# Forgetting attention and SiLU feed-forward on one core: score matmuls grouped by head pair, and PSUM banks and second-layer pieces reassigned

## The chip, the cores and the metric

The kernel runs on one core of a Trainium2 chip. A core has a matrix engine (TensorE, in profiles PE for matmuls and PEld for weight loads), a vector engine (VectorE, DVE), an activation engine (ScalarE, ACT), GpSimd (POOL), and SyncE (SP), which here only issues DMAs. Each engine works through its own queue in program order and waits on semaphores. Matmul results go to PSUM, eight banks of 128 partitions by 2 KB; all else lies in SBUF.

The metric is device microseconds for one execution, inputs and outputs in DRAM. Less is better. The time before is 346.61 us, the median of 6 runs (345.94 to 347.65).

## The reference, cut to what matters

Batch 8, 8 heads, sequence 576, head size 64; then a feed-forward layer of 512 to 2048 to 512 over all 4608 tokens.

```python
scores = scale * np.matmul(q, k.transpose(0, 1, 3, 2))
log_f = np.log(np.clip(f, 0.0001, 1.0))
cum = np.cumsum(log_f, axis=-1)
decay = cum[:, :, :, None] - cum[:, :, None, :]
scores = np.where(causal, -1000000000.0, scores + decay)
attn = softmax(scores)                      # over the last axis
attn_out = np.matmul(attn, v)
x = attn_out.transpose(0, 2, 1, 3).reshape(B * S, H * D)
h = x @ w_in
out = (h * (1.0 / (1.0 + np.exp(-h)))) @ w_out
```

## The kernel before, in words

**Decay.** The row part of the decay cancels in the softmax, so only a weight by key is left. It is multiplied into v (`convert_v`, on POOL), which has one more column for the denominator.

**Attention units.** A unit `n` is a pair of heads of one batch: 32 units, `NU`. Queries 0 to 127 of every head are done in an opening part (`turn0`, `scores0`, `out0`, `back0`). The pair loop at the end (`for m in range(NQ)`, line 832) does queries 128 to 575, two units an iteration, and it is what the change touches. For a unit, `cast_qk` (POOL) makes bf16 copies, and `transposes` (a DMA transpose on SP's queue) makes `qkT` with head size on the partitions: 64 rows for each of the two heads, so that two score matmuls use the upper and lower half of the array at once ("64*128" in the profile).

**Scores.** The score blocks of a unit are split in three chunks, `CHUNKS[0..2]`, each up to 512 columns a head. A chunk of both heads takes a tile `sc` of two banks of the pool `psc` (2 buffers, so 4 banks). ScalarE takes the exponential into `u`; for chunk 2 also into `ut`, which holds the 64 tail queries. VectorE multiplies the diagonal blocks by the causal masks `tri` (line 469) and `trit` (line 483). In an iteration the chunks come in three groups: `(n,0) (n,1)`, then `(n,2) (n+1,0)`, then `(n+1,1) (n+1,2)`.

**Attention output.** `attend(n)` multiplies `u` and `ut` with v into a tile `dn` of one bank, of the pool `pbig` (4 buffers of one bank); VectorE divides by the denominator into `xr`. `back(m)` turns the two units' `xr` into columns of `x`, by TensorE transposes (`tx`) for the first four pairs and the last, by DMA on SP's queue for the others.

**Feed-forward.** The tokens are split into groups `g` of 256 to 512. M1 chunk `(g, fc)` (`m1_chunk`) is four matmuls into a `pbig` bank `hp`; ScalarE takes the tanh (line 576), VectorE makes `gt` from it and `hp` (line 577), which sets the bank free. M2 piece `(g, tb, part)` (`m2_part`) is four matmuls of 512 columns into a `pbig` bank `po`; four pieces make one tile of 128 tokens, so the bank is held across them. ScalarE copies it to `osb` and POOL's queue stores it. M2 of a group needs all of the group's M1.

**Order.** The order of every engine's work is that of the program text (a manual schedule). Between attention steps, `slot(t)` calls `fill(t)`, which emits M1 and M2 pieces for about `t` us of TensorE work. `step` chooses: it compares how far M1 of the next group and M2 of the present one are, alternates when they are close, and takes M1 first near the end of a group. `two_more` in the opening part also uses `fill`. After each `slot`, `store` issues the outputs of earlier slots. `prepare(n)`, before each of the first two slots, emits the casts, transposes and loads for units `n + 2` and `n + 4`.

The third argument of `fill` before is `least`; its second, `first`, says which kind comes first.

Of the kernel before, what the change touches and what calls it, by code (L numbers as in the profile page):

```python
# [18 lines left out]
def kernel(  # L19
# [22 lines left out]
    RB = NR * P  # L42
# [9 lines left out]
    scale = 1.0 / float(D) ** 0.5  # L52
# [7 lines left out]
    upool = ctx.enter_context(tc.tile_pool(name="upool", bufs=4))  # L60
# [16 lines left out]
    tri = const.tile([P, P], BF16, name="tri")  # L77
# [13 lines left out]
    NG = len(GW)  # L91
# [341 lines left out]
    T0 = P  # L433
# [11 lines left out]
    def scores(n, c):  # L445
        b, p = divmod(n, NP)
        if c == 0:
            us[n] = upool.tile([P, 2, UW], BF16, name="u", tag="u")
        u, ut = us[n], uts[n % 4]
        t = qkT[n]  # L450
        sc = psc.tile([P, 2, SM], FP32, name="sc", tag="sc")
        for kb, q0, q1, o in CHUNKS[c]:
            for i in range(2):
                r = slice(i * D, (i + 1) * D)
                if kb == 0:
                    kt = kT0[b][r, p, :]
                else:
                    k0 = RB if kb == NM else kb * P + RB
                    kt = t[r, k0 : k0 + P]
                nc.tensor.matmul(  # L460
                    sc[:, i, o : o + q1 - q0], lhsT=kt, rhs=t[r, q0:q1], start=True, stop=True
                )
        w = SM if c < 2 else T0
        nc.scalar.activation(  # L464
            out=u[:, :, c * SM : c * SM + w], in_=sc[:, :, 0:w], func=ACT.Exp, scale=scale
        )
        if c == 0:
            x = u[:, :, 0:RB].rearrange("p i (a t) -> p i a t", t=P)
            nc.vector.tensor_tensor(  # L469
                out=x,  # L470
                in0=x,
                in1=tri[:, None, None, :].to_broadcast([P, 2, NR, P]),
                op=ALU.mult,
            )
        if c == 2:
            nc.scalar.activation(  # L476
                out=ut[:, :, 0:3:2, :].rearrange("p k i t -> p i k t"),
                in_=sc[:, :, T0 : T0 + (NM + 1) * ST].rearrange("p i (k t) -> p i k t", t=ST),
                func=ACT.Exp,
                scale=scale,  # L480
            )
            x = ut[:, NM, 0:3:2, :]
            nc.vector.tensor_tensor(  # L483
                out=x, in0=x, in1=trit[:, None, :].to_broadcast([P, 2, ST]), op=ALU.mult
            )

    NGR = 2 * NR + 1

# [2 lines left out]
    def attend(n):  # L491
        b, p = divmod(n, NP)
        if p % 2 == 0:
            xqs[n // 2] = xqp.tile([P, NGR, 2, D], BF16, name="xr", tag="xr", bufs=3)
        xq = xqs[n // 2]
        u, ut = us.pop(n), uts[n % 4]
        dn = pbig.tile([P, NGR, D + 1], FP32, name="dn", tag="big")

        def vals(kb, i):
            h = head(p, i)  # L500
            return v0[b][:, h, :] if kb == 0 else vbf[b][:, kb - 1, h, :]

        for i in range(2):
            for c in range(1, NM):
                for kb in range(c + 1):
                    o = AT[c, kb]
                    nc.tensor.matmul(  # L507
                        dn[:, i * NR + c - 1, :],
                        lhsT=u[:, i, o : o + P],
                        rhs=vals(kb, i),  # L510
                        start=(kb == 0),
                        stop=(kb == c),
                    )
# [117 lines left out]
    M2 = []  # L631
# [4 lines left out]
    at = {"m1": 0, "m2": 0, "left": 0.0, "last": 0, "row": 0}  # L636
    ready: set[int] = set()
    open2 = {"w": False}

    def step():  # L640

        a, c = at["m1"], at["m2"]
        can1 = a < len(M1) and M1[a][0] in ready
        g1 = M1[a][0] if a < len(M1) else NG
        g2 = M2[c][0] if c < len(M2) else NG
        if can1 and M1[a][1] == 0 and g1 > g2 + 1:
            can1 = False
        can2 = open2["w"] and c < len(M2) and g2 < g1
        if not can1 and not can2:
            return None  # L650
        if can1 and can2:
            f1 = M1[a][1] / NFC
            f2 = (c - sum(M2_OF[:g2])) / M2_OF[g2]
            want = 3 - at["last"] if abs(f1 - f2) < 0.15 else (1 if f1 < f2 else 2)
            if want == at["last"] and at["row"] >= 2 and abs(f1 - f2) < 0.25:
                want = 3 - want
            if sum(M2_OF[: g2 + 1]) - c <= 2 and f1 >= 0.75:
                want = 1
            can1 = want == 1
        kind = 1 if can1 else 2  # L660
        at["row"] = at["row"] + 1 if kind == at["last"] else 1
        at["last"] = kind
        if can1:
            m1_chunk(*M1[a])
            at["m1"] += 1
            return 4 * (GW[g1] / 2.4 + 2.5)
        m2_part(*M2[c])
        at["m2"] += 1
        return 4 * (DM / 2.4 + 2.5)
# [6 lines left out]
    def fill(us_, first=0, least=0):  # L676
        if first:
            at["last"], at["row"] = 3 - first, 2
        at["left"] += us_ * 1000
        while at["left"] > 0 or least > 0:  # L680
            t = step()
            if t is None:
                at["left"] = 0.0
                return False
            at["left"] -= t
            least -= 1
        return True

# [79 lines left out]
    def two_more(b, banned):  # L768
        for x in range(2):
            turn0(b + x, 0)  # L770
            turn0(b + x, 1)
            fill(0.6, 0, 1)
        for x in range(2):
            if banned:
                scores0(b + x, ban0(b + x))
            else:
                scores0(b + x)
                mask0(b + x)
            fill(0.6 if x == 0 else 2.0, 2, 1 if x == 0 else 2)
        out0(b)  # L780
        fill(0.6, 0, 1)
        out0(b + 1)
        fill(0.8, 0, 2)
        back0(b, on_act)
        fill(0.6, 0, 1)
        back0(b + 1, on_act)
        fill(0.6, 2, 1)

    fill(5.0)
    two_more(4, True)  # L790
    ready.add(1)
    fill(5.0)
    open2["w"] = True
    fill(6.0, 2)
    two_more(6, False)
    ready.add(2)
    fill(4.0)
# [22 lines left out]
    LAG = 13.0  # L820
    pending: list = []

    def slot(us_, first=0):
        n = len(stores)
        fill(us_, first)
# [66 lines left out]
```

The softmax here doesn't subtract the row's maximum and nothing guards it: scores larger than these inputs give would overflow.

## Time and profile before

| What | Value |
|---|---|
| median of 6 runs | 346.61 us |
| the profiled execution | 345.94 us |
| its span, first to last instruction | 344.2 us |
| mean granted TensorE clock | 0.999 |
| DMA traffic, mean | 147 GB/s |
| M2 matmuls, line 613 | 592, 144.7 us |
| M1 matmuls, line 568 | 832 in all forms |
| pair-loop scores, line 460 | 768 matmuls |
| exponentials of 1024 columns, line 464 | 64, mean 1034 ns |
| tanh of 384 columns, line 576 | 128, mean 503 ns |
| gt of 384 columns, line 577 | 128, mean 553 ns |
| copies po to osb of 512 columns, line 623 | 35, mean 607 ns |
| pair-loop scores, first and last group start | 60.37 and 272.34 us |

The profile is of one execution. The span is 1.7 us shorter than the execution's time, which includes what lies around the instructions. The listed length of a matmul reaches to the end of its pipeline; matmuls overlap, so the time that one takes of TensorE is the difference between its start and that of the next. Instructions of one kind in a row are merged in the timeline, with their count behind an x. In square brackets stands the idle time of the engine before an instruction, and what ended it.

### The profile page before, as it was taken

The numbers are of one execution on the slowest core, as the hardware profiler recorded it, in microseconds if no ns is written. First come the engines' busy times: TensorE is split into PE (matmuls) and PEld (weight loads), VectorE is DVE, ScalarE is ACT, GpSimd is POOL, SyncE is SP. The second block draws the span as 40 slices with busy tenths as digits, with TensorE's granted clock in tenths as the row PEclk, the third lists the DMA queues.
The fourth block names the chain that finished last, engine by engine and source line by source line (L and its number), as shares of the span: only waits on it lengthen the run. The fifth ranks groups of instructions, "written<-read, shape, count | busy, mean of one in ns | idle before, by whom it ended". The sixth has DMA issues, their size and how long they took to land.

```text
span 344.2 us, 8892 instructions
## 1 busy us (share of the span) xinstructions
PE 335.3 (97%) x3567; PEld 199.2 (58%) x3567; DVE 183.7 (53%) x389; ACT 218.1 (63%) x401; POOL 129.5 (38%) x227
## 2 busy tenths in 40 slices
PE   8999999989998999999999999999999999999995
PEld 3754656657655656466465665656656565555664
DVE  4766635465667467367545654546645454535330
ACT  5867555887586766756759667595775934445441
POOL 8996224834526363155127128225320000010011
PEclk9999999999999999999999999999999999999999
DMA  8999999999699897998889799989932000010113
GB/s 152 197 192 218 199 165 159 229 215 196 155 196 195 197 200 155 177 201 182 162 185 175 169 180 196 161 190 173 172 86 57 33 32 30 32 58 28 39 39 85
DMA packets 141497, 50.44 MB, mean 147 GB/s; under 512 B 132368, under 2 KB 138768, under 8 KB 141456
## 3 DMA queue, kind: packets, MB, share of 16 engines
q1 hardware_dynamic: 131440, 32.70, 54.4%
q0 software_dynamic: 9856, 17.04, 21.1%
q8 instruction: 28, 0.46, 0.6%
q10 hardware_dynamic: 160, 0.13, 0.1%
q14 instruction: 13, 0.11, 0.1%
HBM read 36.85 MB, written 9.44 MB: 134 GB/s over the span
## 4 chain that ended last, share of the span: by engine, by line
PE 72%; DMA 15%; SPq 4%; POOL 4%; issue 2%; ACT 1%; DVE 1%; POOLq 0%
PE po L613 30%; PE hp L568 28%; PE sc L460 6%; DMA kf<-in_k_dram 5%; PE dn L507 4%; DMA vf<-in_v_dram 4%; DMA w_out_bf<-in_moe_w_out_dram 3%; PE dn L516 2%; SPq L158 2%; DMA qkb<-in_k_dram 1%; DMA qkT<-qkb 1%; SPq L428 1%; POOL qkb L131 1%; DMA qf<-in_q_dram 1%; POOL v L341 1%
## 5 line engine op out<-in xcount | busy, mean ns | idle before, releaser
L576 ACT ACTIVATE th<-hp 128x384 bf16<-128x384 f32 (+2 forms) x208 | 96.0, 478 | 90.1 <-PE hp L568 86.3
L577 DVE SCALAR_TENSOR_TENSOR gt<-th,hp 128x384 bf16<-128x384 bf16 (+2 forms) x208 | 105.9, 522 | 80.1 <-ACT th L576 76.6
L613 PE MATMUL po<-w_out_bf,gt 128*128 128x512 bf16 (+1 forms) x592 | 144.7, 374 | 0.0
L568 PE MATMUL hp<-x,w_in_bf 128*128 128x384 bf16 (+2 forms) x704 | 128.9, 321 | 0.2
L568 PEld LDWEIGHTS <-w_in_bf 128*128 128x128 bf16 x832 | 78.5, 98 | 55.2 <-issue 2.2
L613 PEld LDWEIGHTS <-gt 128*128 128x128 bf16 x592 | 54.6, 98 | 49.6 <-issue 2.1
L464 ACT ACTIVATE u<-sc 128x1024 bf16<-128x1024 f32 (+1 forms) x96 | 75.1, 821 | 11.4 <-PE sc L460 11.3
L592 POOL DMA_DIRECT2D out_dram<-osb x38 | 21.0, 552 | 130.3 <-ACT osb L623 83.2
L414 POOL TENSOR_TENSOR vp<-vf,w_bf 128x520 bf16<-128x520 f32 (+1 forms) x32 | 34.0, 1065 | 30.8 <-DMA vf<-in_v_dram 29.6
L469 DVE TENSOR_TENSOR u<-u,tri 128x768 bf16<-128x768 bf16 x32 | 22.4, 699 | 19.1 <-ACT u L464 19.1
L400 POOL CAST qkb<-qf 128x384 bf16<-128x384 f32 x32 | 17.7, 552 | 32.8 <-DMA qf<-in_q_dram 31.8
L623 ACT ACTIVATE osb<-po 128x512 f32<-128x512 f32 (+1 forms) x37 | 22.0, 595 | 12.3 <-PE po L613 12.2
L483 DVE TENSOR_TENSOR ut<-ut,trit 128x128 bf16<-128x128 bf16 x32 | 10.6, 332 | 34.5 <-ACT ut L476 34.5
L460 PE MATMUL sc<-qkT 64*128 64x128 bf16 (+1 forms) x640 | 26.5, 207 | 1.4 <-DMA qkT<-qkb 1.4
L460 PEld LDWEIGHTS <-qkT 64*128 64x128 bf16 x640 | 18.2, 94 | 12.5 <-issue 9.4
L476 ACT ACTIVATE ut<-sc 128x640 bf16<-128x640 f32 x32 | 23.3, 727 | 0.0
L507 PEld LDWEIGHTS <-u 128*128 128x128 bf16 x576 | 20.7, 98 | 3.5 <-issue 1.2
L507 PE MATMUL dn<-vp,u 128*128 128x65 bf16 x384 | 21.8, 193 | 0.0
L507 PE MATMUL dn<-v,u 128*128 128x65 bf16 x192 | 19.8, 193 | 0.9 <-DVE gt L577 0.9
L525 DVE TENSOR_TENSOR xr<-dn,rec 128x448 bf16<-128x448 f32 x32 | 20.0, 625 | 1.1
L400 POOL CAST qkb<-kf 128x384 bf16<-128x384 f32 x32 | 17.1, 534 | 8.9 <-DMA kf<-in_k_dram 8.9
L568 PE MATMUL hp<-xt,w_in_bf 128*128 128x256 bf16 x128 | 18.2, 272 | 0.3 <-DVE gt L577 0.2
(68 smaller groups left out, 204.6 us busy)
## 6 DMA issues: line engine op xcount, KB each, us to landing
out_dram<-osb POOLq DMA_DIRECT2D x32, 256.0 KB, 2.9
vf<-in_v_dram SPq DMA_DIRECT2D x26, 256.0 KB, 5.0
qf<-in_q_dram SPq DMA_DIRECT2D x64, 96.0 KB, 2.8
kf<-in_k_dram SPq DMA_DIRECT2D x64, 96.0 KB, 2.8
w_in_bf<-in_moe_w_in_dram POOLq DMA_DIRECT2D x4, 512.0 KB, 6.9
w_out_bf<-in_moe_w_out_dram POOLq DMA_DIRECT2D x4, 512.0 KB, 9.2
vf<-in_v_dram POOLq DMA_DIRECT2D x6, 256.0 KB, 9.6
qkb<-in_q_dram POOLq DMA_DIRECT2D x8, 128.0 KB, 4.9
```

The source lines that it names most:

```text
L400: nc.gpsimd.tensor_copy(out=t2[:, c0 : c0 + NR, :].rearrange("p c x -> p (c x)"), in_=t[:, :, :, :].rearrange("p c h d -> p (c h d)"),)
L414: nc.gpsimd.tensor_tensor(out=vbf[b][r, c, :, :], in0=vst[b][c][r, :, :], in1=w_bf[r, c + 1, b * H : (b + 1) * H, None].to_broadcast([n, H ...
L460: nc.tensor.matmul(sc[:, i, o : o + q1 - q0], lhsT=kt, rhs=t[r, q0:q1], start=True, stop=True)
L464: nc.scalar.activation(out=u[:, :, c * SM : c * SM + w], in_=sc[:, :, 0:w], func=ACT.Exp, scale=scale)
L469: nc.vector.tensor_tensor(out=x, in0=x, in1=tri[:, None, None, :].to_broadcast([P, 2, NR, P]), op=ALU.mult,)
L476: nc.scalar.activation(out=ut[:, :, 0:3:2, :].rearrange("p k i t -> p i k t"), in_=sc[:, :, T0 : T0 + (NM + 1) * ST].rearrange("p i (k t) ...
L507: nc.tensor.matmul(dn[:, i * NR + c - 1, :], lhsT=u[:, i, o : o + P], rhs=vals(kb, i), start=(kb == 0), stop=(kb == c),)
L568: nc.tensor.matmul(hp[:, :], lhsT=w_in_bf[:, cc, fc * P : (fc + 1) * P], rhs=xcols(g, cc), start=(cc == 0), stop=(cc == NCC - 1),)
L576: nc.scalar.activation(out=th[:, :], in_=hp[:, :], func=ACT.Tanh, scale=0.5)
L577: nc.vector.scalar_tensor_tensor(out=gt[:, fc, :], in0=th[:, :], scalar=1.0, in1=hp[:, :], op0=ALU.add, op1=ALU.mult,)
L613: nc.tensor.matmul(po[:, :], lhsT=gt[:, fc, tb * P : (tb + 1) * P], rhs=w_out_bf[:, fc, m0:m1], start=(fc == 0), stop=(fc == NFC - 1),)
L623: nc.scalar.activation(out=osb[:, :], in_=po[:, :], func=ACT.Copy, scale=0.5)
```

## The change

There are three edits in the pair loop and in the choice of feed-forward pieces.

1. **Scores.** All three chunks of a unit are emitted in one group, in the order 0, 2, 1. Chunk 1 goes to two single-bank `pbig` tiles (`sb`), one a head, with an exponential of 512 columns for each. The exponentials of chunk 2 and the tail mask are postponed (`late`): they are emitted after the first M1 chunk, or the second piece, of the next slot.
2. **Attention output.** `dn` lies in a `psc` buffer (two banks, of which it uses the first) rather than in a `pbig` one. Between `attend(n)` and `attend(n + 1)` there is now a slot of 0.7 us.
3. **Filling.** `wanted` compares M1 and M2 progress within M1 of the group, from where M2 stood when that M1 began, and so spreads M2 evenly. `fill` plans a slot's kinds first; with `ends` it puts an M2 piece at the slot's start or end (or both), and spreads the rest between. The slots of an iteration change from three of 2.4 us (1.7 in the first two iterations) and one of up to 3.5 to two of 3.4 (2.2), one of 0.7 and one of up to 3.0.

The numbers of matmuls, their sizes, the loads, casts and stores stay.

```diff
+    late: list = []
+
+    def scores(n):
         b, p = divmod(n, NP)
-        if c == 0:
-            us[n] = upool.tile([P, 2, UW], BF16, name="u", tag="u")
+        us[n] = upool.tile([P, 2, UW], BF16, name="u", tag="u")
         u, ut = us[n], uts[n % 4]
         t = qkT[n]
-        sc = psc.tile([P, 2, SM], FP32, name="sc", tag="sc")
-        for kb, q0, q1, o in CHUNKS[c]:
+        sc = {}
+        for c in (0, 2, 1):
+            if c == 1:
+                sc[c] = [pbig.tile([P, SM], FP32, name="sb", tag="big") for _ in range(2)]
+            else:
+                sc[c] = psc.tile([P, 2, SM], FP32, name="sc", tag="sc")
+            for kb, q0, q1, o in CHUNKS[c]:
...
+            if c == 0:
+                nc.scalar.activation(
+                    out=u[:, :, 0:SM], in_=sc[c][:, :, :], func=ACT.Exp, scale=scale
                 )
...
+            if c == 1:
+                for i in range(2):
+                    nc.scalar.activation(
+                        out=u[:, i, SM : 2 * SM], in_=sc[c][i][:, :], func=ACT.Exp, scale=scale
+                    )
+
+        def rest():
+            x = sc[2]
+            nc.scalar.activation(
+                out=u[:, :, 2 * SM : UW], in_=x[:, :, 0:T0], func=ACT.Exp, scale=scale
+            )
             nc.scalar.activation(
                 out=ut[:, :, 0:3:2, :].rearrange("p k i t -> p i k t"),
...
+        late.append(rest)
...
-        dn = pbig.tile([P, NGR, D + 1], FP32, name="dn", tag="big")
+        dn_ = psc.tile([P, 2, SM], FP32, name="dn", tag="sc")
+        dn = dn_[:, 0, 0 : NGR * (D + 1)].rearrange("p (c d) -> p c d", d=D + 1)
...
+    def wanted(a, c):
+        g1 = M1[a][0] if a < len(M1) else NG
+        g2 = M2[c][0] if c < len(M2) else NG
+        can1 = g1 in ready and not (M1[a][1] == 0 and g1 > g2 + 1)
+        can2 = open2["w"] and c < len(M2) and g2 < g1
+        if not can1 or not can2:
+            return 1 if can1 else 2 if can2 else 0
+        a0, c0 = begin.get(g1, (M1[a][1], c)) if M1[a][1] else (0, c)
+        c1 = sum(M2_OF[:g1])
+        f1 = (M1[a][1] - a0 + 0.5) / (NFC - a0)
+        f2 = (c - c0 + 0.5) / max(1, c1 - c0)
+        return 1 if f1 <= f2 else 2
...
+        at["n"] += 1
+        if kind == 1 or at["n"] == 2:
+            while late:
+                late.pop(0)()
+        return t
...
+    def fill(us_, least=0, ends=(0, 0)):
+        left = us_ + at["left"]
+        kinds = plan(left)
+        n2 = kinds.count(2)
+        kinds += [0] * (least - len(kinds))
+        if any(ends) and n2 and 0 not in kinds:
+            e0 = 1 if ends[0] else 0
+            e1 = 1 if ends[1] and n2 > e0 else 0
+            n1, mid = len(kinds) - n2, []
+            inner = n2 - e0 - e1
+            for x in range(n1 + inner):
+                mid.append(2 if (x + 1) * inner // (n1 + inner) > x * inner // (n1 + inner) else 1)
...
+            kinds = [2] * e0 + mid + [2] * e1
...
     for m in range(NQ):
         n = 2 * m
-        piece = 1.7 if m < 2 else 2.4
-        scores(n, 0)
-        scores(n, 1)
+        piece = 2.2 if m < 2 else 3.4
+        scores(n)
         prepare(n)
-        slot(piece, 2)
+        slot(piece, 1, 1)
...
-        scores(n, 2)
-        scores(n + 1, 0)
+        scores(n + 1)
         prepare(n + 1)
-        slot(piece, 2)
-        scores(n + 1, 1)
-        scores(n + 1, 2)
-        slot(piece, 2)
+        slot(piece, 1, 0)
         attend(n)
+        slot(0.7)
         attend(n + 1)
-        slot(min(3.5, max(0.8, behind() - LAG)) if m > 1 else 0.8, 1)
+        slot(min(3.0, max(0.6, behind() - LAG)) if m > 1 else 0.9, 0, 1)
```

More of the change, by code (lines that the diff above doesn't have):

```diff
@@ L443 @@
     AT |= {(2, 1): RB, (3, 1): SM + RB, (3, 2): 2 * SM}
-    def scores(n, c):
+    late: list = []
+    def scores(n):
         b, p = divmod(n, NP)
-        if c == 0:
-            us[n] = upool.tile([P, 2, UW], BF16, name="u", tag="u")
+        us[n] = upool.tile([P, 2, UW], BF16, name="u", tag="u")
         u, ut = us[n], uts[n % 4]
         t = qkT[n]
-        sc = psc.tile([P, 2, SM], FP32, name="sc", tag="sc")
-        for kb, q0, q1, o in CHUNKS[c]:
[L453 to L461, printed above, removed]
-                )
[L463 to L473, printed above, removed]
@@ new lines, in scores @@
+        sc = {}
[6 more added lines that the diff above has]
+                for i in range(2):
+                    r = slice(i * D, (i + 1) * D)
+                    if kb == 0:
+                        kt = kT0[b][r, p, :]
+                    else:
+                        k0 = RB if kb == NM else kb * P + RB
+                        kt = t[r, k0 : k0 + P]
+                    x = sc[c][i] if c == 1 else sc[c][:, i, :]
+                    nc.tensor.matmul(
+                        x[:, o : o + q1 - q0], lhsT=kt, rhs=t[r, q0:q1], start=True, stop=True
+                    )
+            if c == 0:
+                nc.scalar.activation(
+                    out=u[:, :, 0:SM], in_=sc[c][:, :, :], func=ACT.Exp, scale=scale
+                )
+                x = u[:, :, 0:RB].rearrange("p i (a t) -> p i a t", t=P)
+                nc.vector.tensor_tensor(
+                    out=x,
+                    in0=x,
+                    in1=tri[:, None, None, :].to_broadcast([P, 2, NR, P]),
+                    op=ALU.mult,
+                )
+            if c == 1:
+                for i in range(2):
+                    nc.scalar.activation(
+                        out=u[:, i, SM : 2 * SM], in_=sc[c][i][:, :], func=ACT.Exp, scale=scale
+                    )
@@ L474, in scores @@
+        def rest():
+            x = sc[2]
+            nc.scalar.activation(
+                out=u[:, :, 2 * SM : UW], in_=x[:, :, 0:T0], func=ACT.Exp, scale=scale
             )
[L475 removed]
             nc.scalar.activation(
                 out=ut[:, :, 0:3:2, :].rearrange("p k i t -> p i k t"),
[L478 removed]
+                in_=x[:, :, T0 : T0 + (NM + 1) * ST].rearrange("p i (k t) -> p i k t", t=ST),
@@ L635 @@
     M2_OF = [sum(1 for x in M2 if x[0] == g) for g in range(NG)]
-    at = {"m1": 0, "m2": 0, "left": 0.0, "last": 0, "row": 0}
+    at = {"m1": 0, "m2": 0, "left": 0.0, "n": 0}
     ready: set[int] = set()
     open2 = {"w": False}
-    def step():
-        a, c = at["m1"], at["m2"]
-        can1 = a < len(M1) and M1[a][0] in ready
+    begin: dict[int, tuple[int, int]] = {}
+    def wanted(a, c):
         g1 = M1[a][0] if a < len(M1) else NG
         g2 = M2[c][0] if c < len(M2) else NG
-        if can1 and M1[a][1] == 0 and g1 > g2 + 1:
-            can1 = False
+        can1 = g1 in ready and not (M1[a][1] == 0 and g1 > g2 + 1)
@@ L648, in step @@
         can2 = open2["w"] and c < len(M2) and g2 < g1
-        if not can1 and not can2:
-            return None
[L651 to L664, printed above, removed]
-            at["m1"] += 1
[L666 to L669, printed above, removed]
+        if not can1 or not can2:
+            return 1 if can1 else 2 if can2 else 0
+        a0, c0 = begin.get(g1, (M1[a][1], c)) if M1[a][1] else (0, c)
+        c1 = sum(M2_OF[:g1])
@@ new lines, in wanted, with step @@
+        f1 = (M1[a][1] - a0 + 0.5) / (NFC - a0)
+        f2 = (c - c0 + 0.5) / max(1, c1 - c0)
+        return 1 if f1 <= f2 else 2
+    def step(force=0):
+        a, c = at["m1"], at["m2"]
+        want = wanted(a, c)
+        if not want:
+            return None
+        g1 = M1[a][0] if a < len(M1) else NG
+        g2 = M2[c][0] if c < len(M2) else NG
+        can1 = g1 in ready and not (M1[a][1] == 0 and g1 > g2 + 1)
+        can2 = open2["w"] and c < len(M2) and g2 < g1
+        kind = force if (force == 1 and can1) or (force == 2 and can2) else want
+        if kind == 1:
+            if M1[a][1] == 0:
+                begin[g1] = (0, c)
+            m1_chunk(g1, M1[a][1])
+            at["m1"] += 1
+            t = 4 * (GW[g1] / 2.4 + 2.5)
+        else:
+            m2_part(*M2[c])
+            at["m2"] += 1
+            t = 4 * (DM / 2.4 + 2.5)
+        at["n"] += 1
[3 more added lines that the diff above has]
+        return t
@@ L674, in behind, with plan @@
         return t / 1000
[L676 to L681, printed above, removed]
+    def plan(us_):
+        a, c, kinds = at["m1"], at["m2"], []
+        while us_ > 0:
+            k = wanted(a, c)
+            if not k:
+                break
+            kinds.append(k)
+            if k == 1 and M1[a][1] == 0:
+                begin[M1[a][0]] = (0, c)
+            us_ -= (4 * (GW[M1[a][0]] / 2.4 + 2.5) if k == 1 else 4 * (DM / 2.4 + 2.5)) / 1000
+            a, c = a + (k == 1), c + (k == 2)
+        return kinds
+    def fill(us_, least=0, ends=(0, 0)):
[10 more added lines that the diff above has]
+                mid.append(2 if (x + 1) * inner // (n1 + inner) > x * inner // (n1 + inner) else 1)
+            if inner and mid[-1] == 2 and e1:
+                mid = mid[::-1] if not (e0 and mid[0] == 2) else mid
+            kinds = [2] * e0 + mid + [2] * e1
+        at["n"] = 0
+        for k in kinds:
+            t = step(k)
             if t is None:
                 at["left"] = 0.0
[L684 to L687, printed above, removed]
+                return
+            left -= t / 1000
+        at["left"] = left
     on_act, on_dve = nc.scalar.copy, nc.vector.tensor_copy
@@ L771, in two_more @@
             turn0(b + x, 1)
-            fill(0.6, 0, 1)
+            fill(0.6, 1)
         for x in range(2):
@@ L778, in two_more @@
                 mask0(b + x)
-            fill(0.6 if x == 0 else 2.0, 2, 1 if x == 0 else 2)
+            fill(0.6 if x == 0 else 2.0, 1 if x == 0 else 2)
         out0(b)
-        fill(0.6, 0, 1)
+        fill(0.6, 1)
         out0(b + 1)
-        fill(0.8, 0, 2)
+        fill(0.8, 2)
         back0(b, on_act)
-        fill(0.6, 0, 1)
+        fill(0.6, 1)
         back0(b + 1, on_act)
-        fill(0.6, 2, 1)
+        fill(0.6, 1)
     fill(5.0)
@@ L793 @@
     open2["w"] = True
-    fill(6.0, 2)
+    begin[M1[at["m1"]][0]] = (M1[at["m1"]][1], at["m2"])
+    fill(6.0)
     two_more(6, False)
@@ L821, with slot @@
     pending: list = []
-    def slot(us_, first=0):
+    def slot(us_, *ends):
         n = len(stores)
-        fill(us_, first)
+        fill(us_, 0, ends)
+        while late:
+            late.pop(0)()
         store(n)
```

## The prediction

> **What bounds the kernel now.** I read the engine shares first, then the list of waits, then the timeline of TensorE and of ScalarE over one head pair of units in the middle (160 to 178 us), then the waits of TensorE one by one. The page opens with this:
>
> ```profile
> PE 335.3 (97%) x3567; PEld 199.2 (58%) x3567; DVE 183.7 (53%) x389; ACT 218.1 (63%) x401; POOL 129.5 (38%) x227
> ...
> PE 72%; DMA 15%; SPq 4%; POOL 4%; issue 2%; ACT 1%; DVE 1%; POOLq 0%
> ```
>
> TensorE is busy 97% of the span and the granted clock is full throughout, so the question is what its time consists of. The timeline of TensorE (start, length, line, operation; matmuls merged) shows it:
>
> ```profile
> 164.00 1.46 PE L568 MATMUL hp<-x,w_in_bf 128*128 128x384 bf16 x8
> 165.39 0.40 PE L460 MATMUL sc<-qkT 64*128 64x128 bf16 x8
> 165.63 0.33 PE L460 MATMUL sc<-qkT,kT 64*128 64x384 bf16 x2
> 165.79 0.22 PE L460 MATMUL sc<-qkT 64*128 64x128 bf16 x2
> 165.94 2.12 PE L568 MATMUL hp<-x,w_in_bf 128*128 128x384 bf16 x12
> 167.90 1.03 PE L613 MATMUL po<-w_out_bf,gt 128*128 128x512 bf16 x4
> 168.86 0.23 PE L460 MATMUL sc<-qkT 64*128 64x128 bf16 x2
> ```
>
> Take differences of starts. The twelve hp matmuls take 1.96 us, 0.163 each, which is 384 columns at 2.35 columns a ns: M1 and M2 run at the array's rate. The eight before the scores should take 1.31 and take 1.39. The four po take 0.96 before the scores at 168.86 (against 0.86 elsewhere). The last pair of scores at 165.79 holds the array 0.15 until hp starts, where four equal pairs at 165.39 took 0.24, 0.06 each. So **a group of scores, which uses the array as two halves of 64 rows, costs about 0.1 us on entry and 0.1 on exit**. Over all 48 score groups of the pair loop the medians, from the starts of neighbouring matmuls less their columns at 2.4 per ns, are 98 and 95 ns: 0.193 us a group, 9.3 us in all. Attention outputs (dn) are full-height and cost nothing of this.
>
> Real waits of TensorE in the pair loop are few:
>
> ```profile
> 74.23 0.40 PE L460 MATMUL sc<-qkT 64*128 64x128 bf16 x8 [1.01 <-DMA qkT<-qkb]
> ```
> ```profile
> PE sc L460 <- DMA qkT<-qkb: 1.4, 2, 1.0
> ...
> PE dn L507 <- DVE gt L577: 0.9, 1, 0.9
> ```
> ```profile
> 105.14 1.51 DVE L483 TENSOR_TENSOR ut<-ut,trit 128x128 bf16<-128x128 bf16 x1 [1.23 <-ACT ut L476]
> ```
>
> Twice the scores wait for a transposed qkT (units 3 and 5, at 73 and 85 us; with the lesser wait some 1.4 us). Once dn waits for its PSUM bank, because it takes a general bank that an M1 chunk has still to leave, and the VectorE mask ahead of that chunk took 1.51 us instead of 0.23. A smaller stretch of the same sort stands at 216 us (0.3).
>
> **The change, part by part.**
>
> *Grouping.* The order in which the two programs are built has the same 768 score matmuls, in 32 groups instead of 48. Sixteen groups fewer at 0.193 us is **3.1 us**. All of it is on the path, since TensorE waits for nothing else there. The Trainium skill ("TensorEngine Tiling (Array Packing)", Key Properties) says that changing the tiling mode drains the array, and "TensorE: Matmul & The Clock Gate" (Single matmul latency) puts the constant part of a lone matmul at 166 ns warm; a full drain on each side would be an estimate of 0.33 us a group and 5.3 us. The rows say 0.193 for both sides together, so I take 3.1.
>
> *Splitting the attention outputs* with a 0.7 us slot between: at 160.78 us, 56 dn matmuls take 1.70 us with po before and hp after, and no gap on either side; nothing.
>
> *dn in score banks.* dn no longer waits for a general bank, so the 0.93 us at 107 us and the 0.3 at 216 go: **gain 1.2**. What is late next are the M1 chunks queued on the same VectorE, below.
>
> *ScalarE.* The general-bank chunk has two exponentials of 512 columns instead of one of 1024. Back to back in the trace a 1024 one holds ScalarE 0.90 us, a 512-column one 0.49; that adds 0.08 a unit, 2.6 us in all on an engine that is busy 63%. It costs only through lateness.
>
> *The general banks.* This is the price. There are four; M2 holds one across four pieces, the score group now takes two, and until the exponentials have read them one is left for M1. I walk one group through with the row lengths (start of group 0; matmul result usable 0.17 after the last issue):
> - TensorE: scores to 0.75, po piece to 1.61, hp to 2.26, 2.91, 3.56.
> - ScalarE: exp of chunk 0 at 0.43, first half of the general chunk 1.33 to 1.93, second 1.81 to 2.41, tanh 2.45 to 2.94, then the postponed 0.26 and 0.59 us exponentials, done at 3.8, then tanh ending 4.18, 4.57.
> - VectorE: gt of the three chunks done at 3.5, 4.75, 5.25.
>
> The second hp needs the first half's bank (1.93, wanted 2.26) and the third the second's (2.41, wanted 2.91): no stall. The next group comes at 4.5 behind a po piece, its general chunk at 4.97, and needs the second hp's bank, free at 4.75: no stall, 0.2 to spare. Where the built order has four hp chunks and no po piece before the next group (three places), the next general chunk is wanted at 4.75 and its bank is free at 5.1: 0.4 each. Once four hp chunks are followed by a tx transpose, wanted at 4.2, bank free at 4.75: 0.6. Twice a single hp chunk stands between dn and the next group (early, where little M1 work is ready), so the score bank that dn holds comes late: 0.4 each. Sum 1.2 + 0.6 + 0.8 = 2.6. VectorE's slow masks (mean 332 ns against 230 at best) now meet banks with 0.2 us to spare; I add 0.4. **Loss 3.0**, bounds 0.5 (stalls swallowed by later slack) and 8 (a stall of 0.3 in each of 27 groups).
>
> *The early pair loop.* The units' transposes come at times that DMA and SP's queue set: unit 5's is issued at 81.16 behind four loads of v (77.08 to 81.05), and SP's order does not change. So TensorE again waits for unit 3 and is released at the same time. In the built order one M1 chunk more stands before unit 3's scores and three more before unit 5's (four hp of 256 columns each, 0.44 a chunk): at unit 5's release 1.3 us more work is done. Unit 5 is then reached at about 85.4, when its transpose (landed 85.2) is there. Short slots of the first two pairs give waits of about 0.6 for the postponed exponentials, mostly hidden under unit 3's wait; I take 0.4 as uncovered. Two of the 16 saved groups lie before this point and only change waiting (0.4). Net gain 1.3 - 0.15 - 0.4 - 0.4, about **0.4**.
>
> *Even spreading of M2* changes the order, not the number, of full-height matmuls; from hp to po costs 0.01 to 0.02 us. Its use is in the bank distances above. SP and POOL keep the same order of loads, casts and transposes; qkT buffers come free sooner. From unit 7 on transposes land over 2 us before use, later 10, which covers 3 us of a faster TensorE.
>
> **Sum.** 3.1 + 1.2 + 0.4 - 3.0 = 1.7 us, with the stall bounds at hand -3.3 to +4.2. The profiled execution took 345.94 us (span 344.2 and 1.7 around it); that becomes 344.2. It is the fastest of six, 0.67 below their median 346.61, so for a median I take **344.7**.
>
> **Rivals.**
> - *The banks hold (faster, more).* Stalls shrink to 0.5: 346.6 - 4.2 = 342.4. For it: the walk shows a steady pair without a stall, ScalarE's 63%. Against: spare times of 0.2 us.
> - *M1 starves of banks (slower).* The place is the M1 chunks after each score group, where one general bank of four is free and the tanh queues behind exponentials; the price is a wait of TensorE per group. Gains are 4.7 in all, so over the 27 groups after unit 5 it decides from 0.17 us a group. At 0.25 the time is 346.6 + 6.75 - 4.7 = 348.7. For it: ScalarE waits 86.3 us for hp in the list of waits, so its work comes in bursts, and each group makes a burst of 2 us in front of a tanh. Against: the slots start with M2, which needs no new bank.
> - *No change.* DMA is over 85% busy until 240 us; if the input stream, not TensorE, set the pace again at each unit, all savings would turn into waits: 346.6. Against: only two waits for qkT stand in the trace, both before 86 us.
>
> **Numbers.** A difference under 0.2% (0.7 us) can't be told from no change. Forecast 0.50 (343.2 to 345.9), banks hold 0.20, starving 0.18, no change 0.12. Faster by more than 0.2% (below 345.9): 0.70; within: 0.12; slower: 0.18. The range reaches into both sides: 341.8 to 348.0.
>
> **What would show it.** 32 score groups with entry and exit still near 0.1 us; no dn waiting for gt; waits of hp or sb for DVE gt or ACT u of some 3 us in all, at places with four hp chunks in a row; the wait for unit 3 still there, that for unit 5 gone. It is wrong if entry or exit grows, if waits for PSUM banks sum to over 5 us, or if waits for qkT appear after 100 us.

## The result, and the profile after

The changed kernel takes **348.87 us** (median of 34 runs) where the kernel before takes 347.31 (71 runs, taken beside it): a ratio of **1.005, 95% interval 1.0036 to 1.0063**. It is slower by some 1.7 us, and the prediction had 344.7. Single executions that ran well above the rest of their kernel are left out of the ratios (three of six in run 3).

The page of the changed kernel has these two lines for the engine shares and for the chain that ended last:

```profile
PE 335.4 (97%) x3567; PEld 200.2 (58%) x3567; DVE 184.7 (53%) x389; ACT 219.9 (63%) x433; POOL 129.4 (37%) x227
...
PE 80%; ACT 8%; DVE 6%; issue 2%; DMA 2%; POOL 1%; POOLq 0%
```

TensorE is as busy as before, but the chain now runs through ScalarE and VectorE for 14% of the span; before it did for 2%. The chain is work that others waited for: exponentials, tanh and gt have become late. Its span is 346.8 us against 344.2.

The 16 groups were saved as planned. The timeline of TensorE in the changed kernel (start, length, line, operation, count) has two score groups, one without and one with a wait:

```profile
153.33 0.45 PE L469 MATMUL sc<-qkT 64*128 64x128 bf16 x10
153.62 0.19 PE L469 MATMUL sc<-qkT,kT 64*128 64x64 bf16 x2
153.65 0.28 PE L469 MATMUL sc<-qkT 64*128 64x64 bf16 x8
153.77 0.33 PE L469 MATMUL sb<-qkT,kT 64*128 64x384 bf16 x2
153.93 0.22 PE L469 MATMUL sb<-qkT 64*128 64x128 bf16 x2
154.08 1.04 PE L634 MATMUL po<-w_out_bf,gt 128*128 128x512 bf16 x4
154.96 2.76 PE L589 MATMUL hp<-x,w_in_bf 128*128 128x384 bf16 x16
157.65 0.45 PE L469 MATMUL sc<-qkT 64*128 64x128 bf16 x10
157.94 0.19 PE L469 MATMUL sc<-qkT,kT 64*128 64x64 bf16 x2
157.97 0.28 PE L469 MATMUL sc<-qkT 64*128 64x64 bf16 x8
158.09 0.32 PE L469 MATMUL sb<-qkT,kT 64*128 64x384 bf16 x1
158.75 0.32 PE L469 MATMUL sb<-qkT,kT 64*128 64x384 bf16 x1 [0.34 <-DVE gt L598]
158.76 0.37 PE L469 MATMUL sb<-qkT 64*128 64x128 bf16 x2
159.22 1.02 PE L634 MATMUL po<-w_out_bf,gt 128*128 128x512 bf16 x4
```

The first group lasts 154.08 - 153.33 = 0.75 us, the second 159.22 - 157.65 = 1.57: it waits 0.8 us. Of this, 0.66 lies between the two `sb` matmuls of 384 columns (158.09 and 158.75), which start together in the first group, and 0.15 in front of po. The bracket says 0.34 for the first and nothing for the second: the `sb` matmul at 158.09 is listed with 0.32 us, and idle time is counted from there. Differences of starts are the safe reading here too.

Over all 32 groups, the time beyond 0.75 us sums to 7.5 us; before, two of 48 groups waited, 1.7 in all. Waits elsewhere from 36 us on (dn, tx, hp) come to 2.1 us against 2.0; in the changed kernel 0.6 of it is a tx transpose's wait for a general bank. Entry is still 98 ns and exit 95. With the small gaps inside them, a group costs 0.235 us beyond its columns against 0.224 before, so the groups cost 32 x 0.235 = 7.5 us instead of 48 x 0.224 = 10.75. The balance is (7.5 - 1.7) + (2.1 - 2.0) - (10.75 - 7.5) = 5.8 + 0.1 - 3.2 = +2.7 us, beside 2.6 between the two spans.

The list of waits of the changed kernel names what ended the waits (total, times, longest, in us; as idle time is counted from the listed ends, these are too short):

```profile
PE sc L469 <- ACT ut L494: 2.1, 3, 1.1
...
PE sb L469 <- DVE gt L598: 0.8, 2, 0.5
PE dn L360 <- DVE u L336: 0.5, 1, 0.5
PE sc L469 <- DVE xr L546: 0.5, 2, 0.3
```

By differences of starts the 7.5 us divide into some 4.1 for a general bank (sb, or the po behind it, waiting for VectorE's gt), 2.6 for the postponed exponential of the tail chunk (ACT ut), and 0.85 for the score bank that dn still holds (DVE xr). All three are waits for a PSUM bank.

ScalarE's timeline in the changed kernel, in front of the 0.8 us wait, shows how a bank comes to be late:

```profile
153.77 1.02 ACT L473 ACTIVATE u<-sc 128x1024 bf16<-128x1024 f32 x1 [0.71 <-PE sc L469]
154.69 1.08 ACT L485 ACTIVATE u<-sb 128x512 bf16<-128x512 f32 x2
155.65 0.62 ACT L644 ACTIVATE osb<-po 128x512 f32<-128x512 f32 x1
156.13 0.52 ACT L597 ACTIVATE th<-hp 128x384 bf16<-128x384 f32 x1
156.50 0.43 ACT L491 ACTIVATE u<-sc 128x256 bf16<-128x256 f32 x1
156.76 0.76 ACT L494 ACTIVATE ut<-sc 128x640 bf16<-128x640 f32 x1
157.34 1.33 ACT L597 ACTIVATE th<-hp 128x384 bf16<-128x384 f32 x3
```
```profile
155.97 2.18 POOL L414 TENSOR_TENSOR vp<-vf,w_bf 128x520 bf16<-128x520 f32 x2
157.55 0.68 DVE L501 TENSOR_TENSOR ut<-ut,trit 128x128 bf16<-128x128 bf16 x1 [0.32 <-ACT ut L494]
158.16 1.47 DVE L598 SCALAR_TENSOR_TENSOR gt<-th,hp 128x384 bf16<-128x384 bf16 x3
```

The second tanh of the slot begins at 157.34, behind the group's first three exponentials, a copy of po, the first tanh and the two postponed exponentials. VectorE's tail mask, which comes before the second gt in its queue, takes 0.68 us (0.23 at best), and the second gt of the slot, the one that frees the bank, ends near 158.7. TensorE wanted that bank at 158.1.

Two things in this queue are worth a closer look. The first is the copy of po (`osb`), which stands there only where the slot's first piece ends a tile of 128 tokens. Two slots with the same TensorE work, one with it and one without, show its price; in both the mask takes 0.23 us:

```profile
168.87 1.08 ACT L485 ACTIVATE u<-sb 128x512 bf16<-128x512 f32 x2
169.82 0.62 ACT L644 ACTIVATE osb<-po 128x512 f32<-128x512 f32 x1
170.30 0.52 ACT L597 ACTIVATE th<-hp 128x384 bf16<-128x384 f32 x1
172.11 1.02 DVE L598 SCALAR_TENSOR_TENSOR gt<-th,hp 128x384 bf16<-128x384 bf16 x2 [0.16 <-ACT th L597]
```
```profile
226.44 1.08 ACT L485 ACTIVATE u<-sb 128x512 bf16<-128x512 f32 x2
227.56 0.49 ACT L597 ACTIVATE th<-hp 128x384 bf16<-128x384 f32 x1
229.33 1.02 DVE L598 SCALAR_TENSOR_TENSOR gt<-th,hp 128x384 bf16<-128x384 bf16 x2 [0.16 <-ACT th L597]
```

The groups before them begin at 167.50 and 225.08. The second gt (the first of these two) begins 4.61 us after the one and 4.25 after the other and ends 0.55 later, at 5.16 and 4.80. The next group wants the bank at 4.97: it waits 0.24 us in the first case and nothing in the second.

The second is the mask. Of the 32 tail masks of the changed kernel 23 take 0.22 to 0.23 us, and the other nine (up to 1.13) all end 0.08 to 0.09 us after a cast or multiplication of POOL ends; here POOL's at 155.97 ends at 158.15 and the mask at 158.24. The six slow masks of the kernel before do the same. A mask that begins while POOL works seems to be held until that is done; no run moves POOL's work to test it. Here it costs less than the copy: the second tanh ends at 157.90, so the second gt, which begins at 158.16, lost some 0.2 us.

### The profile page after: what moved, and what is told of

Same layout as the page of the kernel before. It is cut to its first block, busy times and chain, and to the rows that moved or that the text cites. A ratio compares the mean times of both kernels' runs of the same rounds, so it can differ in the third digit from the quotient of the medians.

```text
span 346.8 us, 8937 instructions
## 1 busy us (share of the span) xinstructions
PE 335.4 (97%) x3567; PEld 200.2 (58%) x3567; DVE 184.7 (53%) x389; ACT 219.9 (63%) x433; POOL 129.4 (37%) x227
## 4 chain that ended last, share of the span: by engine, by line
PE 80%; ACT 8%; DVE 6%; issue 2%; DMA 2%; POOL 1%; POOLq 0%
PE po L634 34%; PE hp L589 29%; PE dn L528 5%; PE sc L469 3%; DVE gt L598 3%; PE dn L537 3%; ACT u L485 2%; PE sb L469 2%; PE tp L286 2%; DMA vf<-in_v_dram 2%; ACT th L597 2%; PE wm L232 1%; ACT u L473 1%; ACT ut L494 1%; ACT u L491 1%
## 5 line engine op out<-in xcount | busy, mean ns | idle before, releaser
L589 PE MATMUL hp<-x,w_in_bf 128*128 128x384 bf16 (+2 forms) x704 | 125.7, 321 | 0.3
L473 ACT ACTIVATE u<-sc 128x1024 bf16<-128x1024 f32 x32 | 33.3, 1041 | 13.3 <-PE sc L469 13.3
L485 ACT ACTIVATE u<-sb 128x512 bf16<-128x512 f32 x64 | 35.3, 619 | 0.0
L469 PEld LDWEIGHTS <-qkT 64*128 64x128 bf16 x640 | 17.3, 94 | 17.0 <-issue 14.1
L528 PEld LDWEIGHTS <-u 128*128 128x128 bf16 x576 | 21.6, 98 | 5.1
L469 PE MATMUL sc<-qkT 64*128 64x128 bf16 (+1 forms) x576 | 20.0, 206 | 2.6 <-ACT ut L494 2.1
```

The source lines that it names most:

```text
L469: nc.tensor.matmul(x[:, o : o + q1 - q0], lhsT=kt, rhs=t[r, q0:q1], start=True, stop=True)
L473: nc.scalar.activation(out=u[:, :, 0:SM], in_=sc[c][:, :, :], func=ACT.Exp, scale=scale)
L485: nc.scalar.activation(out=u[:, i, SM : 2 * SM], in_=sc[c][i][:, :], func=ACT.Exp, scale=scale)
L528: nc.tensor.matmul(dn[:, i * NR + c - 1, :], lhsT=u[:, i, o : o + P], rhs=vals(kb, i), start=(kb == 0), stop=(kb == c),)
L589: nc.tensor.matmul(hp[:, :], lhsT=w_in_bf[:, cc, fc * P : (fc + 1) * P], rhs=xcols(g, cc), start=(cc == 0), stop=(cc == NCC - 1),)
```

## The experiments

All ratios are to the kernel before, run beside each kernel. "The changed kernel" stands at 1.005. All twelve traces lack 47 to 50 of the 3567 matmul records; a gap of about 0.2 us where one is missing is not a wait, and I leave it out. Waits below are from differences of starts, with the releaser from the trace. "Waits of groups" are what score groups last beyond 0.75 us.

**1. Longer early slots.**

```diff
-        piece = 2.2 if m < 2 else 3.4
+        piece = 3.4
```

> The changed kernel with slots of 3.4 us in the first two iterations too (instead of 2.2). Theory A (TensorE waits because the two general banks and the postponed exponentials of a score group come free too late): the waits of the scores of units 1 and 3 for the exponential of the tail chunk, 1.3 and 0.9 us in the changed kernel's trace, go; unit 3 may wait for its transpose no longer than in the kernel before; time 1.0 to 2.0 us below the changed kernel's 348.9, so 347 to 348. Rival B (the even spreading of M2 or the opening part is what costs): no more than 0.5 us moves. Rival C (a merged score group is itself slower than three split ones): no more than 0.5 us moves.

Measured: 1.0056 (1.0035 to 1.0076), so no gain; theory A's time was missed. The waits for ACT ut are gone altogether, as it said, but others have grown. The list of waits of this run has:

```profile
PE sb L469 <- DVE gt L598: 1.4, 3, 0.8
...
PE sc L469 <- DVE xr L546: 1.1, 3, 0.6
PE hp L589 <- DVE gt L598: 0.8, 2, 0.4
```

The early slots use up M2 pieces; the next slots are then filled with up to five M1 chunks in a row, each with a tanh and a gt, and banks come late there. Removing one wait by moving pieces made another.

**2. Tail exponentials not postponed.**

```diff
-        late.append(rest)
+        rest()
```

> The changed kernel with the exponentials of the tail chunk emitted at once behind those of the general chunk, ahead of the first tanh. Theory A: the scores' waits for the tail exponential shrink (they come 0.5 us sooner), but each tanh comes 0.65 us later, so the waits of sb for a general bank grow; time within 1.5 us of the changed kernel, the mix of waits shifted from ACT ut to DVE gt. Rival B and C: no change of the mix and of the time.

Measured: 1.0113 (1.0082 to 1.0145), some 2 us slower than the changed kernel (1 to 3.4 by the intervals; up to 1.5 was expected). The mix shifts as theory A says: waits for ACT ut 2.6 to 0.7 us, waits of hp for a bank (DVE gt) 0.7 to 3.1. New are eight waits of 0.28 us each for the copy of po (ACT osb), which now stands behind all exponentials. Postponing them was right; the tanh is the more urgent of the two.

**3. dn back in a general bank.**

```diff
-        dn_ = psc.tile([P, 2, SM], FP32, name="dn", tag="sc")
-        dn = dn_[:, 0, 0 : NGR * (D + 1)].rearrange("p (c d) -> p c d", d=D + 1)
+        dn = pbig.tile([P, NGR, D + 1], FP32, name="dn", tag="big")
```

> The changed kernel with dn back in a general bank, as before. Theory A: two more tenants for the four general banks in each iteration, so waits for DVE gt grow; 1 to 3 us slower than the changed kernel, while the waits of scores for DVE xr (0.37 and 0.46 us) go. If moving dn was a loss by itself (a rival reading of those two waits), the kernel is faster than the changed one by about 0.8 us.

Measured: 1.010 (1.0057 to 1.0144), slower than the changed kernel by some 0.5%. The interval is wide and touches the changed kernel's, so this is a direction, not a size. The trace is of an execution of 354.9 us, 4.4 above the 350.5 us behind the ratio, and gives no size either. In it the waits of scores for DVE xr are gone and dn waits 0.8 us for gt; one wait of po of 3 us stands behind a tail mask of 3.39 us, which ends 0.09 us after POOL's work does. Nothing here makes moving dn a loss.

**4. The new choice of pieces alone,** with the old grouping.

> The kernel before (three score groups an iteration, dn in a general bank, no postponed exponentials) with the changed kernel's choice of pieces alone, in the opening part too. Theory A: the spreading by itself does no harm; within 0.7 us of the kernel before, apart from the wait of 0.7 us in the opening part (dn of batch 7 for its mask). Rival B: the kernel is slower by most of the 1.6 us that the whole change costs.

```diff
     def slot(us_, first=0):
         n = len(stores)
-        fill(us_, first)
+        fill(us_, 0, (first == 2, first == 1))
```

(and `step`, `fill`, `wanted`, `plan` and the opening's calls as in the changed kernel). Measured: 0.9982 (0.9964 to 1.000): no slower than before, so rival B falls. Its opening has waits of its own: dn waits 1.4 and 0.3 us near 54 and 55 us, ended by POOL's conversion of v, not by the mask that ends the changed kernel's. Yet the kernel is no slower: unit 3 waits for its DMA transpose for 0.9 us instead of 1.2, and unit 5 not at all instead of 0.5, so half of the lost time was spare.

**5 and 6. Both kernels without tanh and multiply.**

```diff
-        th = tpool.tile([P, w], BF16, name="th", tag="th")
-        nc.scalar.activation(out=th[:, :], in_=hp[:, :], func=ACT.Tanh, scale=0.5)
-        nc.vector.scalar_tensor_tensor(
...
+        nc.vector.tensor_copy(out=gt[:, fc, :], in_=hp[:, :])
```

> The kernel before without the SiLU: ScalarE's tanh and the multiply are left out, and VectorE copies hp to gt at once, so that an M1 chunk's bank comes free one copy after its matmuls and ScalarE loses 95 us of work. All theories: TensorE's stream is the same, so within 0 to 3 us below the kernel before (its one wait of dn for gt goes).

> The changed kernel with the same part left out (no tanh, no multiply; VectorE copies hp to gt). Theory A: with the tanh no longer queued behind the exponentials, the waits of TensorE for general banks and for the tail exponential go, and the 16 saved groups show: 2.5 to 4.5 us faster than the kernel before without the SiLU. Rival B (even spreading or the opening part): still 1 to 2 us slower than it. Rival C (merged groups are no cheaper): within 1 us of it.

Measured: the kernel before 1.0004 (0.9984 to 1.0024), 346.97 us; the changed kernel **0.9921 (0.9892 to 0.9951)**, 344.23 us. This test decides between the theories. With the chain from hp to a free bank shortened to one copy, the old order gains nothing, and the new one turns from 1.7 us slower to 2.7 us faster. Rivals B and C fall: the merged groups are cheaper by about what the sum said, and what eats it is the lateness of banks. The edit shortens ScalarE's queue and VectorE's at once and so does not part the two. Waits remain, and theory A's "go" was too much: groups still wait 1.3 us for ACT ut and 2.2 for gt (4.1 in the changed kernel), nearly all of the 2.2 in slots with masks of 0.3 to 1.2 us.

**7. Twice as many score groups.**

```diff
         scores(n, 0)
+        fill(piece / 2, 2)
         scores(n, 1)
         prepare(n)
-        slot(piece, 2)
+        slot(piece / 2, 2)
```

(and so for the other two groups of an iteration).

> The kernel before with a piece of M1 or M2 between any two chunks of scores: 96 groups instead of 48. If entry and exit of a score group cost 0.19 to 0.22 us each time and lie on the path: 9 to 11 us slower than before, with 98 ns on entry and about 95 on exit in the trace. If the gap is hidden or belongs to something else: less than 3 us slower.

Measured: 1.0191 (1.0162 to 1.022), 6.6 us slower: below the 9 to 11 expected. The price is as expected. TensorE's timeline of this run shows one chunk between full-height pieces:

```profile
160.03 1.47 PE L568 MATMUL hp<-x,w_in_bf 128*128 128x384 bf16 x8
161.44 0.23 PE L460 MATMUL sc<-qkT 64*128 64x128 bf16 x2
161.50 0.19 PE L460 MATMUL sc<-qkT,kT 64*128 64x64 bf16 x2
161.53 0.28 PE L460 MATMUL sc<-qkT 64*128 64x64 bf16 x8
161.75 1.04 PE L613 MATMUL po<-w_out_bf,gt 128*128 128x512 bf16 x4
162.62 0.81 PE L568 MATMUL hp<-x,w_in_bf 128*128 128x384 bf16 x4
```

Eight hp take 1.41 instead of 1.31 before the group. Over the 96 groups entry is 99 ns and exit 95 in the median, so 48 more cost 9.3 us. Against that, waits from 17 us on fall from 5.0 us to 1.7: neither scores for their transposes (1.7) nor dn for its bank (1.1) wait any more. 9.3 - 3.3 = 6.0, near the 6.6 measured. Cheaper switching and easier timing pull against each other, the same trade as in the change, run backwards.

**8. The split exponential alone,** in the kernel before.

```diff
+        for i in ((slice(0, 1), slice(1, 2)) if c == 1 else (slice(0, 2),)):
             nc.scalar.activation(
-                out=u[:, :, c * SM : c * SM + w], in_=sc[:, :, 0:w], func=ACT.Exp, scale=scale
+                out=u[:, i, c * SM : c * SM + w], in_=sc[:, i, 0:w], func=ACT.Exp, scale=scale
             )
```

> The kernel before with the exponential of chunk 1 as two of 512 columns instead of one of 1024. Theory A: ScalarE's work grows by 3 us in all, but no bank is shorter for it; within 0.7 us of before. If the split is itself what costs in the changed kernel: 1 us or more slower.

Measured: 1.0014 (0.9993 to 1.0034), at most a small loss. The split itself is not the cause.

**9 to 12. Repairs that follow from theory A.** In run 9 the postponed exponentials come after the second M1 chunk of a slot (`k1` counts them):

```diff
-        if kind == 1 or at["n"] == 2:
+        at["k1"] += kind == 1
+        if at["k1"] == 2 or at["n"] == (3 if at["k1"] else 2):
             while late:
                 late.pop(0)()
```

> The changed kernel with the postponed exponentials one step later: after the second M1 chunk of a slot rather than after the first, so that the tanh of the second chunk, on which a general bank of the next score group hangs, comes 0.8 us sooner. Theory A: the waits of sb for DVE gt (1.7 us in the changed kernel's trace, with those of the po behind them 2.6) shrink by half or more in the later iterations, the waits for ACT ut of units 1 and 3 grow by up to 0.8 us each; in all 0.5 to 2 us faster than the changed kernel. Without the bank chain as the cause: no change within 0.5 us.

Measured: 1.0036 (1.0021 to 1.005), 0.5 us faster than the changed kernel, at the lower end of what was expected, and the intervals overlap. The waits of groups for a general bank fall from 4.1 to 2.9 us, those for ACT ut grow from 2.6 to 3.8: in sum nothing, and what is gained is the wait of tx (0.6). In the early iterations the postponed exponentials now come too late.

Run 10 also holds the slots' ends:

```diff
+        if any(ends) and len(kinds) > sum(ends) and 0 not in kinds and 5 <= M1[at["m1"]][0]:
+            while kinds.count(2) < sum(ends):
+                kinds[len(kinds) - 1 - kinds[::-1].index(1)] = 2
```

> As the run before, and from the fifth M1 group on a slot that is to begin and end with an M2 piece does so even where the even spread would give it one M2 piece less (three hp chunks and a po, not four hp chunks, stand before the next score group). Theory A: the waits of sb for DVE gt go almost wholly after 150 us; 1.5 to 3 us faster than the changed kernel, at or below the kernel before (0.995 to 1.000).

Measured: **0.9975 (0.9959 to 0.9991)**, 346.09 us, 2.6 us faster than the changed kernel. The waits of groups for a general bank are down to some 1 us from 4.1, of which 0.8 is at one place, unit 7 at 104 us; after 150 us hardly any is left, as expected. Those for ACT ut stay, at 3.3.

Run 11 is the changed kernel with the opening part filled by the old choice of pieces.

> The changed kernel with the opening part filled as before (the old choice of pieces up to the pair loop), the pair loop as changed. If the opening's order costs what the traces show at 40 to 55 us: 0.7 us faster than the changed kernel, with the wait of dn for the mask at 54 us gone and those in the pair loop the same. If that wait is covered by the later wait for DMA: no change.

Measured: 1.0011 (0.9993 to 1.0029), 1.3 us faster than the changed kernel (0.6 to 2.1 by the intervals; 0.7 was expected). The wait of dn for the mask is down from 0.7 to 0.2. By the pieces that the old opening leaves over, most of the waits for ACT ut are gone too (2.6 to 0.9): the first slot now has three M2 pieces (2.6 us) where the changed kernel has one piece and two short M1 chunks (1.8 us), so unit 1 comes some 0.8 us later after unit 0's exponentials. Unit 3 again waits for its transpose (0.45).

Run 12 is all three.

> All three: the opening as before, the postponed exponentials after the second M1 chunk, and the slots' ends held. Theory A: the savings of the 16 groups now exceed what waits are left; 344.5 to 346.5 us, or 0.992 to 0.998 of the kernel before.

Measured: **0.9924 (0.9899 to 0.9949), 344.7 us**: faster than both kernels. The waits of groups are down from 7.5 us to 2.9, with 0.7 for a transpose in front of unit 3; the two ratios differ by 4.4 us. The timeline of TensorE in this run, at the place shown above:

```profile
154.15 2.11 PE L589 MATMUL hp<-x,w_in_bf 128*128 128x384 bf16 x12
156.10 1.03 PE L634 MATMUL po<-w_out_bf,gt 128*128 128x512 bf16 x4
157.06 0.45 PE L469 MATMUL sc<-qkT 64*128 64x128 bf16 x10
...
157.49 0.33 PE L469 MATMUL sb<-qkT,kT 64*128 64x384 bf16 x2
157.65 0.22 PE L469 MATMUL sb<-qkT 64*128 64x128 bf16 x2
```

Three hp chunks and a po stand before the group instead of four hp, and the sb matmuls follow each other without a wait. The second tanh stands ahead of the postponed exponentials and the mask, so slow masks (0.57 us in this slot) no longer hold its bank.

## Why the prediction was wrong, point by point

Two steps failed. In the walk that priced the general banks, ScalarE's list had no copy of po, and in the early pair loop waits were put at 0.4 us that came to over 2. The sum was +1.7 us of gain; the two traces say -2.6, which is 4.3 less. Waits for banks from unit 5 on came to 5.3 us (4.7 inside groups, 0.6 before tx) where 3.0 stood, and the early loop, with its two saved groups, to -1.5 where +0.8 stood: 2.3 and 2.3, about the whole.

- **The gain of 16 groups** (3.1 us): right. 3.2 in the trace, entry and exit unchanged, and run 7 shows the price from the other side. The measured price was the right choice over the prediction's estimate of a full drain on each side, which would have made it 5.3.
- **dn in score banks** (gain 1.2): right; dn no longer waits for gt, and runs 3 and 8 give no sign that this or the split exponential costs. (The lesser of the two stretches, near 217 us, was a wait of hp and not of dn; it is down from 0.4 us to 0.1.)
- **The general banks** (loss 3.0 with dn's bank and VectorE's slow masks): the mechanism was right and the sizes were too small. dn's bank cost 0.85 where I had 0.8, and the tx transpose 0.6 as worked out. But two places with four hp chunks cost 0.8 and 0.9 and the third 0.5, where I had 0.4 each. And the steady slot, for which I found 0.2 us to spare and put nothing, waits 0.24 at three places and 0.4 at a fourth. With smaller waits at units 3, 19 and 23 that is 4.1 us for gt instead of 1.2, against which the 0.4 that I put for slow masks was too little. The walk's second gt of the steady slot, at 4.75 us, is what units 25 and 31 show (4.80), where no copy of po stands before the first tanh. At the four places it stands there. At three of them the masks are at their best (0.22 to 0.23) and the second gt ends at 5.16, so it is the copy that turned the spare time into a wait. A slow mask (0.64 us) adds to it at the fourth; both are met at two of the places with four hp chunks, too.
- **The early pair loop** (net gain 0.4, with the two saved groups 0.8): this step failed. I let the waits for the postponed exponentials hide under unit 3's wait for its DMA transpose. There were two of them one after the other, each longer than the 0.6 that I had worked out, and a wait in the opening came before them: the timeline of TensorE in the changed kernel has

```profile
54.12 0.43 PE L360 MATMUL dn<-v,u 128*128 128x65 bf16 x8 [0.53 <-DVE u L336]
65.56 0.23 PE L469 MATMUL sc<-qkT 64*128 64x128 bf16 x2 [1.14 <-ACT ut L494]
76.37 0.23 PE L469 MATMUL sc<-qkT 64*128 64x128 bf16 x2 [0.75 <-ACT ut L494]
```

  The opening's 0.7 and unit 1's 1.3 delayed unit 3 by more than the 1.2 us that its wait for DMA could cover: the transpose landed at 74.75 (74.19 before), the scores began at 75.22, and they then waited another 0.9 for ut. Some 1.5 us were lost (the changed kernel's lag at equal matmul work, with 60 to 80 us of it done).
- **Even spreading of M2** (nothing): right for the pair loop (run 4), wrong for the opening, where one 0.44 us chunk instead of a 0.86 us piece stands between two dn and leaves VectorE's mask uncovered. In run 4, with the old pair loop, the same opening cost no time; with the new one, run 11 gives for the old opening, with what follows from it, 1.3 us.
- **The rivals.** "M1 starves of banks" is what happened: over the 27 groups from unit 5 on, the waits inside score groups sum to 4.7 us, 0.17 a group, just what it takes to eat the gains of 4.7; 3.9 of it is for general banks, and the lost early gain makes the rest of the loss. The place was one step off: not the M1 chunks behind a group wait, but the next group's own sb matmuls, and po behind them. I gave 348.7 to this case, at a chance of 0.18, and 348.9 came; that the figures are so near is luck, since 348.7 stood for 0.25 us a group. My own sign that the forecast is wrong, over 5 us of waits for PSUM banks, came too: 7.5 inside the groups. The evidence was at hand: 35 copies of po of 0.6 us on ScalarE's queue, and a spare time of 0.2 us in a walk without them.

What stays open: how much of the 1.3 us of run 11 is the mask's wait and how much the rearranged first slots, since both moved at once. No run takes the copy of po or POOL's work out of the way, so their prices are read from traces alone.

## What to carry to other kernels

A switch of the matrix array between full height and two halves can have a price that is read from starts of neighbouring instructions (0.19 us in and out here, with 32, 48 and 96 groups alike). Merging such groups saves it, but concentrates what the groups ask of other engines and of buffers. So walk the burst through every queue with everything that stands in it, copies included, and count a spare time as a wait when it is shorter than an instruction that may slip in. When a saving vanishes, shorten the suspected chain in both versions and compare the two: if the new order then wins, repair its timing and keep it. A wait that covers others covers them once; add up everything that is to hide under it.

## What the runs showed of the hardware that was not expected

A VectorE mask of 128 x 128 bf16 elements takes 0.23 us, but up to 1.13 in the changed kernel and 1.51 in the kernel before when it meets work of POOL: all fifteen slow masks of the two traces end 0.08 to 0.09 us after a cast or multiplication of POOL. The idle time that the profile puts in brackets for a matmul can be half of what the starts show (0.34 against 0.66 at 158 us), or be missing (0.15 in front of po).
